# One load of local V, masks first, and rows fetched earlier in a fused sparse-attention and MoE kernel

## The chip, the cores and the metric

The kernel runs on one core of a Trainium2 chip. The metric is device time in microseconds (us) of that core, lower is better. The engines are named as the profile names them: PE (matmul), PEld (its weight load), DVE (VectorE), ACT (ScalarE), POOL (GpSimd) and SP (SyncE, which here only issues transfers). Spans and positions in time come from one profiled execution of each kernel; the time of an execution is 1.7 to 2.0 us longer than its span.

## The reference, cut to what matters

```python
def _attn_ref(q, k, v):                       # each 8 x 8 x 576 x 64, fp32
    scores = scale * q @ k.T
    mask_local   = (rel >= 0) & (rel < 32)    # heads 0 to 3; rel = query - key
    mask_strided = (rel >= 0) & (key % 32 == query % 32)      # heads 4 to 7
    ... softmax over the allowed keys, times v

def _moe_ref(x, w_in, w_out):                 # x: 4608 x 512, d_ff 2048
    r = np.maximum(x @ w_in, 0.0)
    return (r * r) @ w_out
```

Attention of batch b makes 576 rows of x. The 4608 rows of x then go through two matmuls in nine chunks of 512 rows. "MM1 of chunk c" is x @ w_in, "MM2 of chunk c" is the second product. MM1 of chunk c needs the attention of batches up to c, so attention of batch c + 1 is woven between the matmuls of chunk c.

## The kernel before

Heads are handled in pairs, called units: of each batch's four, two are local and two strided. A local unit reads keys in six windows of 128 that overlap by 32. Local V is fetched by POOL's DMAs as those windows, the overlap rows twice:

```python
def load_v_local(u):                          # three DMAs a unit, fp32 to bf16 on the way
    t = vls[v_slot(u)]
    nc.gpsimd.dma_start(out=t[:, :, 0, 0:D], in_=v[b, 2*p:2*p+2, 0:128, :]...)
    for hh in range(2):
        win = bass.AP(src.tensor, src.offset + 64 * D, [[D, 128], [QL * D, NL - 1], [1, D]])
        nc.gpsimd.dma_start(out=t[:, hh, 1:NL, 0:D], in_=win)
```

The rows of q and k of local units come by SP in fp32 and are cast by POOL; those of strided units come by POOL's own DMAs. After the exponential a mask product clears what is not allowed. MM1 ends in a relu on ACT and a square on DVE. These three lines (225, 297 and 188 of the changed kernel) return in the argument:

```python
eng.tensor_tensor(x, x, m..., op=ALU.mult)                 # e <- e, mask: two SBUF inputs
nc.vector.tensor_tensor(g[:, ff, :], r, r, op=ALU.mult)    # square: two SBUF inputs
nc.vector.tensor_copy(o, i)                                # kT <- pt: the transposed k, from PSUM
```

The order of the work is fixed by the program. In the opening:

```python
for n, fn in enumerate(first):          # attention of batch 0
    ...                                 # near its end: rows of batch 1 on ACT's queue
    fn(); tick()
load_v_local(4); cast_qk_local(4, pool2)     # batch 1, on POOL
... load_qk_str(6); load_qk_str(7) ...
for i in range(4): load_w_out(i)
```

and in the stream, a list of groups of four matmuls, into which attention steps and loads are woven:

```python
for c in range(2): all 16 groups of MM1 of chunk c
16 groups of MM2 of chunk 0
for c in range(2, 9): MM1 of chunk c and MM2 of chunk c-1, one group of each in turn
16 groups of MM2 of chunk 8
load_at = {(starts[b - 2] + starts[b - 1]) // 2: b for b in range(2, B)}
```

The softmax here doesn't subtract the row's maximum and nothing guards it: scores larger than these inputs give would overflow.

## Time and profile before

| kernel before | value |
|---|---|
| time, median (lowest to highest of four runs) | 380.87 us (380.09 to 382.98) |
| span of the profiled execution (its time: 381.99 us) | 380.3 us |
| PE busy | 322.9 us, 85% of the span |
| first MM1 of chunk 0 starts at | 33.91 us |
| first MM2 of chunk 1 starts at | 111.55 us |
| from there to the end | 268.8 us |
| mean granted clock | 0.968 |

The two positions are the marks that the rest of this text uses. Up to the second the kernel is opening and start-up; from it on the program repeats one pattern per batch, so the remainder of the span is the steady part plus a tail without attention. The slices, the stretches, the chain and the order of time that carry the reading stand in the prediction. How to read them: a digit of the slices is the busy share of a 40th of the span in tenths, and in the row PEclk the clock granted to PE in tenths of full speed; a row of the stretches gives the stretch, its length, and the busy time of each engine in it; in the order of time a bracket at the end of a row is how long the engine had idled before it, and for what.

One more row of the page, on the transfers:

```profile
DMA packets 50592, 36.10 MB, mean 95 GB/s; under 512 B 28800, under 2 KB 43648, under 8 KB 50560
```

### The profile page before, as it was taken

Reading aid. Unit: us, or ns where it says so; the run is one execution under the profiler, and the core shown is the slowest. Engines: PE = TensorE matmul, PEld = TensorE weight load, DVE = VectorE, ACT = ScalarE, POOL = GpSimd, SP = SyncE. Lnnn points to the kernel's source line nnn. Section 1 sums busy time; section 2 is a strip of 40 time slices with the busy share of each in tenths; the row PEclk is TensorE's granted clock in tenths of the full one; section 3 lists DMA queues with packets and bytes.
Section 4 is the critical chain, followed back from the end, with each engine's and each line's share of the span. In section 5 each row is a group of like instructions: output and inputs, shape, how many; then the busy total and the mean of one; then the engine's idle time right before and its main releaser. Section 6 shows DMA issues by size and latency. Waiting matters only on the chain.

```text
span 380.3 us, 6780 instructions
## 1 busy us (share of the span) xinstructions
PE 322.9 (85%) x2672; PEld 168.3 (44%) x2720; DVE 192.3 (51%) x448; ACT 169.3 (45%) x343; POOL 111.7 (29%) x143
## 2 busy tenths in 40 slices
PE   2277577789999689996999699959999999999995
PEld 1164244345555345543555345534545544444442
DVE  3375458897455447553854386536644632222200
ACT  4231446566335335551555355534555434444421
POOL 8545953991000093007600490019000000000000
PEclk9999779999999989998999899998999999999999
DMA  9999999983110395109800792059100001001012
GB/s 187 122 190 242 197 220 181 184 87 22 57 57 28 98 176 75 47 36 227 94 29 29 204 132 40 29 139 163 55 28 29 29 28 52 33 28 55 29 55 83
DMA packets 50592, 36.10 MB, mean 95 GB/s; under 512 B 28800, under 2 KB 43648, under 8 KB 50560
## 3 DMA queue, kind: packets, MB, share of 16 engines
q0 software_dynamic: 36224, 12.07, 29.0%
q1 hardware_dynamic: 13192, 21.83, 19.5%
q10 hardware_dynamic: 1144, 1.77, 1.9%
q8 instruction: 21, 0.34, 0.4%
q14 instruction: 11, 0.09, 0.1%
HBM read 38.27 MB, written 9.44 MB: 125 GB/s over the span
## 4 chain that ended last, share of the span: by engine, by line
PE 67%; DVE 12%; DMA 11%; ACT 3%; issue 3%; POOL 3%; SPq 0%; POOLq 0%; ACTq 0%
PE ph L284 26%; PE py L299 23%; PE ph L299 7%; DVE g_sb L288 4%; DMA q_st<-in_q_dram 3%; PE pt L167 3%; DMA vl<-in_v_dram 3%; DMA q_s<-in_q_dram 3%; PE pt L202 3%; PE pt L242 3%; ACT r L287 2%; PE pt L265 2%; DMA k_st<-in_k_dram 2%; DVE kT L178 2%; DVE xt L272 2%
## 5 line engine op out<-in xcount | busy, mean ns | idle before, releaser
L284 PE MATMUL ph<-xt,w_in_b 128*128 128x512 bf16 x553 | 150.4, 390 | 3.3 <-DVE xt L272 1.5
L287 ACT ACTIVATE r<-ph 128x512 bf16<-128x512 f32 x144 | 86.1, 598 | 125.5 <-PE ph L284 117.7
L288 DVE TENSOR_TENSOR g_sb<-r 128x512 bf16<-128x512 bf16 x144 | 71.8, 499 | 131.7 <-ACT r L287 131.5
L299 PE MATMUL py<-w_out_b,g_sb 128*128 128x512 bf16 x427 | 114.7, 388 | 1.6 <-issue 0.6
L299 PEld LDWEIGHTS <-g_sb 128*128 128x128 bf16 x576 | 52.2, 99 | 56.2 <-issue 5.0
L284 PEld LDWEIGHTS <-w_in_b 128*128 128x128 bf16 x576 | 51.1, 100 | 48.7 <-issue 4.7
L208 ACT ACTIVATE e<-pt 72x288 bf16<-72x288 f32 (+1 forms) x128 | 48.9, 406 | 29.4 <-PE pt L202 26.4
L91 POOL CAST q_l<-q_st 96x768 bf16<-96x768 f32 x14 | 11.8, 842 | 135.0 <-DMA q_st<-in_q_dram 135.0
L242 PEld LDWEIGHTS <-e 72*128 72x128 bf16 (+1 forms) x448 | 25.8, 104 | 23.5 <-issue 3.3
L176 ACT COPY qT<-pt 128x576 bf16<-128x576 bf16 x32 | 20.4, 637 | 24.5 <-PE pt L167 23.6
L202 PE MATMUL pt<-qT,kT 64*72 64x72 bf16 (+1 forms) x448 | 15.7, 212 | 17.5 <-DVE kT L178 17.0
L118 POOL DMA_DIRECT2D vl<-in_v_dram x32 | 28.4, 897 | 4.4 <-DMA w_out_b<-in_moe_w_out_dram 4.1
L299 PE MATMUL ph<-w_out_b,g_sb 128*128 128x512 bf16 x124 | 29.3, 379 | 0.3
L254 DVE TENSOR_TENSOR x_s<-pt,rinv 72x384 bf16<-72x384 f32 (+1 forms) x48 | 24.5, 509 | 1.7
L167 PE MATMUL pt<-ident,q_l 96*128 96x96 bf16 x96 | 7.8, 225 | 19.8 <-POOL q_l L91 13.6
L202 PEld LDWEIGHTS <-kT 64*72 64x72 bf16 (+1 forms) x448 | 11.1, 111 | 30.1 <-DVE kT L178 24.6
L214 DVE TENSOR_TENSOR e<-e,mask_loc 128x576 bf16<-128x576 bf16 x32 | 19.4, 605 | 7.3 <-POOL mask_loc L392 6.8
L178 DVE COPY kT<-pt 128x576 bf16<-128x576 bf16 x32 | 19.2, 600 | 3.6 <-PE pt L167 3.6
L303 ACT COPY y<-py 128x512 f32<-128x512 f32 x28 | 16.4, 585 | 10.3 <-PE py L299 9.5
L242 PE MATMUL pt<-vs,e 72*128 72x65 bf16 x256 | 16.9, 204 | 2.7 <-DVE e L217 2.7
L131 POOL CAST vs<-v_st 72x1024 bf16<-72x1024 f32 x16 | 18.4, 1174 | 0.0
L254 DVE TENSOR_TENSOR x_l<-pt,rinv 96x384 bf16<-96x384 f32 x32 | 17.7, 553 | 1.1
(43 smaller groups left out, 207.3 us busy)
## 6 DMA issues: line engine op xcount, KB each, us to landing
out_dram<-y SPq DMA_DIRECT2D x36, 256.0 KB
q_st<-in_q_dram SPq DMA_DIRECT2D x14, 288.0 KB
k_st<-in_k_dram SPq DMA_DIRECT2D x14, 288.0 KB
v_st<-in_v_dram SPq DMA_DIRECT2D x14, 288.0 KB
vl<-in_v_dram POOLq DMA_DIRECT2D x32, 80.0 KB, 4.9
q_s<-in_q_dram POOLq DMA_DIRECT2D x16, 144.0 KB, 5.5
k_s<-in_k_dram POOLq DMA_DIRECT2D x16, 144.0 KB, 5.1
w_in_b<-in_moe_w_in_dram POOLq DMA_DIRECT2D x4, 512.0 KB, 7.2
```

The source lines that it names most:

```text
L118: nc.gpsimd.dma_start(out=t[:, hh, 1:NL, 0:D], in_=win)
L176: nc.scalar.copy(o, i)
L178: nc.vector.tensor_copy(o, i)
L202: nc.tensor.matmul(banks[row][half][0:kn, w * i:w * (i + 1)], kT[rows, klo:klo + kn], qT[rows, w * t:w * (t + 1)], start=True, stop=True)
L208: nc.scalar.activation(e[0:kn, lo:lo + S // 2], banks[row][half][0:kn, 0:S // 2], AF.Exp, scale=scale)
L214: nc.vector.tensor_tensor(x, x, mask_loc.rearrange("p t c -> p (t c)"), op=ALU.mult)
L242: nc.tensor.matmul(po[:, n - n0, :], e[0:kn, pos(n):pos(n) + 128], rhs[0:kn, src(n), 0:D + 1], start=True, stop=True)
L254: nc.vector.tensor_tensor(x, po[0:w, 0:m, 0:D], rinv[0:w, 0:m].to_broadcast([w, m, D]), op=ALU.mult)
L284: nc.tensor.matmul(ph, w_in_b[:, kk, 128 * ff:128 * (ff + 1)], xt[kk][:, 512 * c:512 * (c + 1)], start=(kk == 0), stop=(kk == 3))
L287: nc.scalar.activation(r, ph, AF.Relu)
L288: later(1, lambda: nc.vector.tensor_tensor(g[:, ff, :], r, r, op=ALU.mult))
L299: nc.tensor.matmul(py, g[:, ff, 128 * j:128 * (j + 1)], w_out_b[:, ff, :], start=(ff == 0), stop=(ff == 15))
```

## The change: its intent and the diff

Four things are done at once. Local V is loaded once, by SP, in fp32; POOL casts it and copies the 32 overlap rows on chip, so windows become uniform, masks shrink to one narrow tile, and POOL issues fewer DMAs. Masks are built before the casts and weights, and row-0 masks of batch 0 go to POOL, copies and casts of batch 0 to ACT. The rows of a batch are fetched half a chunk pair earlier. And MM2 of chunk 0 goes ahead of MM1 of chunk 1, so that batch 1 has 32 groups of matmuls to hide behind and not 16.

```diff
-    def load_v_local(u):                       # three POOL DMAs
+    def load_v_local(u, eng):
+        t = vl_sts[p]
+        for hh in range(2):
+            eng.dma_start(out=t[32:128, NL * hh:NL * (hh + 1), :],
+                          in_=v[b, 2 * p + hh].rearrange("(t p) d -> p t d", p=QL))
+    def cast_v_local(u):
+        nc.gpsimd.tensor_copy(t[:, :, :, 0:D]..., s["vf"])
+        nc.gpsimd.tensor_copy(t[0:32, :, 1:NL, 0:D], s["vf"][96:128]...[:, :, 0:NL - 1, :])
 ... (keys get 32 zero columns in front: klo = w * t)
         def masks(row):
-            if local: nc.vector.tensor_tensor(x, x, mask_loc...)
-            else:     nc.vector.tensor_tensor(x, x, mask_str.to_broadcast(...))
+            eng = nc.gpsimd if u < 4 and row == 0 else nc.vector
+            eng.tensor_tensor(x, x, m.to_broadcast([kn, n, w]), op=ALU.mult)
 ... (step_E: the xt copies of units 0 to 3 on ACT; casts of units 0 and 1 on ACT)
     def loads(b):
-        load_qk_local, load_v_str; load_v_local(u); cast; load_qk_str(u + 2); load_v_local(u + 1); ...
+        load_qk_local, load_v_local, load_v_str        # all on SP
+        load_qk_str(u + 2); load_qk_str(u + 3)         # POOL issues
+        casts of q, k, local V, strided V              # POOL
 ... (preamble: selects first, then cast_v_local(0), (1), then w_in with strided casts)
-        if n == len(first) - 8: (rows of batch 1 on ACT's queue)
-    load_v_local(4) ... cast_v_str(7)
     for i in range(4):
         load_w_out(i)
+    loads(1)
 ...
-    for i in range(16):
-        add(0, 2, i, ps_h)
+        if c == 0:
+            for i in range(16):
+                add(0, 2, i, ps_h)
-    load_at = {(starts[b - 2] + starts[b - 1]) // 2: b for b in range(2, B)}
+    load_at = {starts[b - 2]: b for b in range(2, B)}
```

More of the change, by code (lines that the diff above doesn't have):

```diff
@@ L59 @@
     ident = singles.tile([128, 128], BF16)
-    mask_loc = singles.tile([128, NL, QL], BF16)
+    mask_loc = singles.tile([128, 1, QL], BF16)
     mask_str = singles.tile([SP_, 1, SP_], BF16)
@@ L63 @@
     vss = [singles.tile([SP_, NBS, VP], BF16, name=f"vs{i}") for i in range(NV)]
+    vl_sts = [singles.tile([128, 2 * NL, D], FP32, name=f"vl_st{i}") for i in range(2)]
+    kTl = [singles.tile([128, 32 + S], BF16, name=f"kTl{i}") for i in range(3)]
     es = [singles.tile([128, 1280], BF16, name=f"e{i}") for i in range(3)]
@@ L106, in v_slot @@
         return (b * 2 + p % 2) % NV
-    def load_v_local(u):
+    def load_v_local(u, eng):
         b, p = units[u]
-        t = vls[v_slot(u)]
-        nc.gpsimd.dma_start(
-            out=t[:, :, 0, 0:D],
-            in_=v[b, 2 * p:2 * p + 2, 0:128, :].rearrange("h p d -> p h d"))
-        for hh in range(2):
-            src = v[b, 2 * p + hh]
-            win = bass.AP(src.tensor, src.offset + 64 * D,
-                          [[D, 128], [QL * D, NL - 1], [1, D]])
-            nc.gpsimd.dma_start(out=t[:, hh, 1:NL, 0:D], in_=win)
-        st.setdefault(u, {})["v"] = t
+        t = vl_sts[p]
+        for hh in range(2):
+            eng.dma_start(out=t[32:128, NL * hh:NL * (hh + 1), :],
+                          in_=v[b, 2 * p + hh].rearrange("(t p) d -> p t d", p=QL))
+        st.setdefault(u, {})["vf"] = t
+    def cast_v_local(u):
+        s = st[u]
+        t = vls[v_slot(u)]
+        nc.gpsimd.tensor_copy(t[:, :, :, 0:D].rearrange("p h t d -> p (h t) d"), s["vf"])
+        nc.gpsimd.tensor_copy(
+            t[0:32, :, 1:NL, 0:D],
+            s["vf"][96:128].rearrange("p (h t) d -> p h t d", h=2)[:, :, 0:NL - 1, :])
+        s["v"] = t
     def load_v_str(u, eng):
@@ L168, in step_T @@
                                 ident[0:w, 0:w])
-        dst = qkT.tile([128, S], BF16, name=f"{name}T")
+        if local and name == "k":
+            full = kTl[u % 3]
+            dst = full[:, 32:32 + S]
+        else:
+            full = dst = qkT.tile([128, S], BF16, name=f"{name}T")
         if local:
@@ L178, in step_T @@
             nc.vector.tensor_copy(o, i)
-        s[name + "T"] = dst
+        s[name + "T"] = full
     def blk_pos(h, j):
@@ L198, in step_S @@
                 t = half * hn + i
-                klo = w * t if not local else max(0, w * t - 32)
+                klo = w * t
                 for row in range(2):
@@ L211, in masks @@
         def masks(row):
-            if local:
-                x = e[:, S * row:S * (row + 1)]
-                nc.vector.tensor_tensor(x, x, mask_loc.rearrange("p t c -> p (t c)"), op=ALU.mult)
-            else:
-                x = e[0:kn, S * row:S * (row + 1)].rearrange("p (t c) -> p t c", c=w)
-                nc.vector.tensor_tensor(x, x, mask_str.to_broadcast([w, n, w]), op=ALU.mult)
+            x = e[0:kn, S * row:S * (row + 1)].rearrange("p (t c) -> p t c", c=w)
+            m = mask_loc if local else mask_str
+            eng = nc.gpsimd if u < 4 and row == 0 else nc.vector
+            eng.tensor_tensor(x, x, m.to_broadcast([kn, n, w]), op=ALU.mult)
         expo(0, 0)
@@ L268, in step_E @@
         dst = xt[p][:, b * S:(b + 1) * S]
+        copy = nc.scalar.copy if u < 4 else nc.vector.tensor_copy
         if local:
-            nc.vector.tensor_copy(dst, px)
+            copy(dst, px)
         else:
-            nc.vector.tensor_copy(dst.rearrange("c (p j) -> c p j", j=NJ),
+            copy(dst.rearrange("c (p j) -> c p j", j=NJ),
                                   px.rearrange("c (j p) -> c p j", j=NJ))
@@ L352, in loads @@
         u = 4 * b
-        load_qk_local(u, nc.sync)
-        load_qk_local(u + 1, nc.sync)
+        for i in range(2):
+            load_qk_local(u + i, nc.sync)
+            load_v_local(u + i, nc.sync)
         load_v_str(u + 2, nc.sync)
         load_v_str(u + 3, nc.sync)
-        load_v_local(u)
-        cast_qk_local(u, pool2)
         load_qk_str(u + 2)
-        load_v_local(u + 1)
-        cast_qk_local(u + 1, pool2)
         load_qk_str(u + 3)
+        for i in range(2):
+            cast_qk_local(u + i, pool2)
+            cast_v_local(u + i)
         cast_v_str(u + 2)
         cast_v_str(u + 3)
-    load_qk_local(0, nc.sync)
-    load_v_local(0)
+    for i in range(2):
+        load_qk_local(i, nc.sync)
+        load_v_local(i, nc.sync)
+    load_qk_str(2)
     make_identity(nc, ident)
-    load_qk_local(1, nc.sync)
-    load_qk_str(2)
     load_v_str(2, nc.sync)
-    load_v_local(1)
     load_v_str(3, nc.sync)
@@ L375 @@
     nc.vector.memset(mask_loc, 1.0)
+    for t in vl_sts:
+        nc.vector.memset(t[0:32], 0.0)
+    for t in kTl:
+        nc.vector.memset(t[:, 0:32], 0.0)
     for t in vls:
         nc.vector.memset(t[:, :, :, D:D + 1], 1.0)
+        nc.vector.memset(t[0:32, :, 0, D:D + 1], 0.0)
     for t in vss:
@@ L381 @@
         nc.vector.memset(e[:, 2 * S:1280], 1.0)
-    tail = mask_loc[:, 1:NL, :]
-    nc.gpsimd.affine_select(out=tail, in_=tail, compare_op=ALU.is_ge, fill=0.0,
-                            base=-1, channel_multiplier=1,
-                            pattern=[[0, NL - 1], [-1, QL]])
-    nc.gpsimd.affine_select(out=tail, in_=tail, compare_op=ALU.is_ge, fill=0.0,
-                            base=32, channel_multiplier=-1,
-                            pattern=[[0, NL - 1], [1, QL]])
-    head = mask_loc[:, 0, :]
-    nc.gpsimd.affine_select(out=head, in_=head, compare_op=ALU.is_ge, fill=0.0,
-                            base=0, channel_multiplier=-1, pattern=[[1, QL]])
-    nc.gpsimd.affine_select(out=head, in_=head, compare_op=ALU.is_ge, fill=0.0,
-                            base=31, channel_multiplier=1, pattern=[[-1, QL]])
+    ml = mask_loc[:, 0, :]
+    nc.gpsimd.affine_select(out=ml, in_=ml, compare_op=ALU.is_ge, fill=0.0,
+                            base=-1, channel_multiplier=1, pattern=[[-1, QL]])
+    nc.gpsimd.affine_select(out=ml, in_=ml, compare_op=ALU.is_ge, fill=0.0,
+                            base=32, channel_multiplier=-1, pattern=[[1, QL]])
     res = singles.tile([SP_, 1, RH], FP32)
@@ L398 @@
                           res.to_broadcast([SP_, NA, RH]))
-    load_w_in(0)
-    cast_v_str(2)
     ms = mask_str[:, 0, :]
@@ L403 @@
                             base=0, channel_multiplier=-1, pattern=[[1, SP_]])
+    cast_v_local(0)
+    cast_v_local(1)
+    load_w_in(0)
+    cast_v_str(2)
     load_w_in(1)
@@ L409 @@
     first = first_steps()
-    cast_qk_local(0, (nc.scalar.copy, nc.vector.tensor_copy))
+    sc2 = (nc.scalar.copy, nc.scalar.copy)
+    cast_qk_local(0, sc2)
     for n, fn in enumerate(first):
         if n == 3:
-            cast_qk_local(1, (nc.scalar.copy, nc.vector.tensor_copy))
-        if n == len(first) - 8:
-            load_qk_local(4, nc.scalar)
-            load_qk_local(5, nc.scalar)
-            load_v_str(6, nc.scalar)
-            load_v_str(7, nc.scalar)
+            cast_qk_local(1, sc2)
         fn()
         tick()
-    load_v_local(4)
-    cast_qk_local(4, pool2)
-    load_v_local(5)
-    cast_qk_local(5, pool2)
-    load_qk_str(6)
-    load_qk_str(7)
-    cast_v_str(6)
-    cast_v_str(7)
     for i in range(4):
         load_w_out(i)
+    loads(1)
     NCH = T // 512
```

## The prediction

> **What bounds the kernel now.** I read the page's slices first, then a table of five stretches, then the chain of waits, then the instructions in order of time around the places where the chain leaves the matmuls. The slices:
>
> ```profile
> PE   2277577789999689996999699959999999999995
> DVE  3375458897455447553854386536644632222200
> PEclk9999779999999989998999899998999999999999
> DMA  9999999983110395109800792059100001001012
> ```
>
> A slice is 9.5 us. The first nine show PE at two to eight tenths with the DMA engines nearly full; after that PE is full but for four slices of 5 or 6 at an even distance, each with a burst of DMA and a clock slice of 8 in it or just behind it. So there are two losses: the opening, and a stall that comes once per batch. The stretches (0 to the first MM1; chunks 0 and 1 of MM1; MM2 of chunk 0; the stream that still carries attention; the stream without it):
>
> ```profile
> core 0: us, PE busy (x) PEld busy (x) DVE busy (x) ACT busy (x) POOL busy (x), PEclk, DMA share, GB/s
> 0.00:33.90 33.90, 14.26 (x196) 10.98 (x198) 18.06 (x52) 10.75 (x23) 19.16 (x32) 1.00 1.12 179
> 33.90:93.20 59.30, 45.57 (x469) 25.35 (x477) 40.81 (x88) 32.30 (x69) 42.30 (x51) 0.91 1.06 159
> 93.20:111.00 17.80, 17.63 (x160) 9.29 (x160) 8.94 (x22) 6.65 (x15) 0.00 (x0) 1.00 0.12 45
> 111.00:307.00 196.00, 176.62 (x1542) 91.52 (x1570) 110.06 (x256) 93.47 (x193) 50.20 (x61) 0.97 0.42 83
> 307.00:380.30 73.30, 68.83 (x313) 31.11 (x318) 14.38 (x33) 26.13 (x44) 0.00 (x0) 1.00 0.12 47
> ```
>
> The last stretch has PE full and no attention in it: a floor that the change doesn't touch. The fourth loses 19.4 us of PE time. The chain names what for:
>
> ```profile
> 129.50 3.29 DMA q_st<-in_q_dram
> 170.04 3.05 DMA q_st<-in_q_dram
> 210.56 3.36 DMA q_st<-in_q_dram
> 251.29 3.25 DMA q_st<-in_q_dram
> ```
>
> Four waits for the first rows of a batch, about 40.5 us apart. The order of time shows how one arises:
>
> ```profile
> 97.92 31.49 SPq L305 DMA_DIRECT2D out_dram<-y  x6
> 129.50 0.38 SPq L83 DMA_DIRECT2D q_st<-in_q_dram  x1
> 132.93 0.81 POOL L91 CAST q_l<-q_st 96x768 bf16<-96x768 f32 x1 [45.65 <-DMA q_st<-in_q_dram]
> 133.80 0.45 PE L167 MATMUL pt<-ident,q_l 96*128 96x96 bf16 x6 [3.45 <-POOL q_l L91]
> ```
>
> The load stands on SP behind stores of y, in program order in the middle of the chunk; the reader should see that POOL had waited 45.65 us, so the cast was ready and the issue was late. In the opening the lines that matter are:
>
> ```profile
> 13.33 0.70 POOL L100 DMA_DIRECT2D k_s<-in_k_dram  x1 [4.09 <-DMA vl<-in_v_dram]
> 15.95 0.46 DVE L214 TENSOR_TENSOR e<-e,mask_loc 128x576 bf16<-128x576 bf16 x1 [6.85 <-POOL mask_loc L392]
> 49.02 0.66 PE L167 MATMUL pt<-ident,q_s 72*128 72x72 bf16 x8 [1.56 <-DMA q_s<-in_q_dram]
> ```
>
> POOL's tenth DMA waits for the second, eight back (local V, in flight from 2.18 to 13.04 us); the masks stand behind it on POOL, and DVE idles 6.85 us for them.
>
> **What the Trainium skill says.** (1) "SBUF — State Buffer", section "Who interferes with whom": a DVE instruction with two SBUF inputs contends with a GpSimd instruction that reads SBUF. The trace agrees: the mask product takes 0.46 us as a rule but 1.89 us at 16.99 and 2.49 us at 65.86 us, both beside POOL casts. (2) "GPSIMD Engine Reference", section 3.1: a two-input elementwise costs about 2.6 cycles per element; at that page's 1.2 GHz, 576 elements make 1.25 us (estimate; before has no such instruction on POOL). (3) "TensorE: Matmul & The Clock Gate", Part 1: after an idle window of about 3.4 us the array runs at half rate. The trace agrees: after the 3.45 us stall the granted clock of 130 to 140 us is 0.83, and matmuls of 512 columns step by about 0.42 instead of 0.216 us. (4) "DMA: Bandwidth & Descriptors", section on queues: each engine consumes a ring in order and takes turns between rings. Before doesn't contradict it; no run isolates it.
>
> **The change, part by part.**
>
> *Rows a chunk ahead.* Loads of batch b move from the middle of the chunk pair to its start, 16 of its 32 matmul groups earlier, so about 17 us earlier. Data, casts and the first transpose take 4.3 us now (129.50 to 133.80). With local V also on SP (two DMAs per unit), the SP burst grows from 6 to 10 issues at about 0.45 us, and POOL first waits a few steps for a free row buffer; call it 10 us together. 17 hides it. One stall costs 3.45 us idle plus the half clock that follows until about 137.6: 3.6 us at half rate, 1.7 us lost, so 5.2 us. Four make 20.8 us. Check: a period is 32 groups x 4 x 0.2155 = 27.6 us, plus a batch's attention on PE. From the chain that is per local unit 0.52 transposes + 0.47 scores + 0.36 + 0.26 = 1.6 us, per strided unit 1.73, so 6.7 us a batch; sum 34.3. Measured: (196.0 - 20.8) / 5 = 35.0. It closes. New stretch: 5 x 35.1 = 175.5 us.
>
> *Opening up to the first MM1 (33.9 now).* Removed from POOL's queue ahead of the masks: the three local-V issues of each of two units (0.87 + 1.77 = 2.6 us a unit) and the 4.09 us wait; the wide selects (0.63 + 0.61) go too. The masks are then ready near 6 instead of 15.9 us. But this is not 10 us won: row-0 masks of units 0 to 3 move to POOL, and there they stand behind all of POOL's preamble: four row issues at 0.73 (2.9), two local-V casts of 0.83 + 0.7 each (3.1, estimated by the q cast of 768 elements), two strided-V casts (2.2), four weight issues (3.1), selects (1.1), so about 12.4 us of work from 1.3 us on, and the casts wait for V: 2.95 MB of batch 0 at about 190 GB/s land by 13 to 15 us. So POOL reaches the first mask at about 20 us and finishes it at 21; now MM of unit 0 starts at 17.72. From there units are faster: DVE loses four masks (1.8 us), four xt copies (2.4) and two casts (1.1) of its roughly 15 us; ACT takes the copies and casts and has about 15 us of work from 2 us on. 21 + 12 = 33 us. I expect 33, a gain of one.
>
> *Stream start.* POOL goes on with four w_out issues, then strided rows of batch 1 (each must wait for the DMA eight back, the w_in loads), then the casts of unit 4. w_in and SP's early loads of batch 1 sum with batch 0 to 7.4 MB, at 205 GB/s 36 us. So the cast comes at about 36 and PE waits some 4 us; strided rows lie in the ring behind 2.1 MB of w_out and cost perhaps 4 more. Then MM1 and MM2 of chunk 0 with batch 1: 34.3 + 2 of small gaps. 33 + 4 + 4 + 36.3 = 77.3 us.
>
> *MM2 first.* Batch 1 gets 32 groups as cover instead of 16, batch 2 gets 16 instead of 32. In MM1 of chunk 1, DVE has 15.1 us for a batch (kT, masks, rinv, x, xt by their rows) + 16 x 0.42 = 21.8, with stretching by POOL 24.5; PE only 20.5. So DVE bounds it: 24.5 us, ending at 101.8. Before, the same work ended at 111.0: 9 us won.
>
> *Copies on chip.* Per batch POOL trades 5.1 us of V issues for 3.1 us of casts; off the path either way.
>
> Sum: 101.8 + 175.5 + 73.3 = 350.6 us of span, and about 1 us from span to time: 352 us.
>
> **Rivals.** (A) POOL becomes the opening's bound: masks at 1.25 us or more, each held by DVE, w_out and casts behind them. For it: POOL's program order and 42.3 of 59.3 us busy already. Against: its work per batch falls. It would make 358 to 366 us. (B) The stalls stay since SP still issues in order, y stores come behind a longer burst, or POOL's row issue waits for a buffer freed late. For: the four stalls are exactly an order problem. Against: 17 us of lead, buffers freed in the first steps of the period. All four kept: 371 us; half of that, 361. (C) w_out is late for MM2 of chunk 0, needed near 57 instead of 93 us (it landed near 65 before, behind small V packets). Up to 8 us more, 360. (D) The opening goes well, batch 1 having arrived long before: no wait at the stream start and the first MM1 near 30: 342.
>
> **Range and chances.** The 20.8 us rest on a wait measured four times; the opening's 9 are a chain of guesses, plus or minus 9. Predicted 352 us, range 344 to 364. Within 2% means above 373.3 us, which needs B in full and nothing won in the opening: faster 0.93, same 0.05, slower 0.02.
>
> **What would show it.** Right: no chain lines of about 3 us for q rows after 100 us; PE slices of 9 there; clock 1.00; first MM1 near 33; MM1 of chunk 2 near 102 with DVE over 85% busy in the stretch before. DVE's 6.85 us for the local mask should be gone, but a wait of PE or DVE for POOL's row-0 mask near 20 us in its place. Wrong: period longer than 36.5 us; PE waiting for w_out; POOL masks far from 1.25 us; first MM1 above 37 or below 29.

## The result, and the profile after

The changed kernel took 365.07 us (median of four runs, 363.83 to 369.91; the last of these counts as slow), the kernel before 380.87. The ratio is 0.957 (95% interval 0.951 to 0.962). Ratios here are the mean time of one kernel's fast runs over that of the other's in the same rounds, so they are not quite the ratio of the medians. Executions over 1.5% slower than the fastest of the same kernel are left out of the means. The kernel is faster, but by 15.8 us where 29 were predicted, and 365.07 lies 1.07 above the upper end of the range.

| | before | predicted | after |
|---|---|---|---|
| first MM1 of chunk 0 | 33.9 | 33 | 36.0 |
| MM1 and MM2 of chunk 0 | | 44.3 | 51.9 |
| MM1 of chunk 1 | | 24.5 | 27.3 |
| start of the steady part | 111.0 | 101.8 | 115.2 |
| five batches of the stream | 196.0 | 175.5 | 175.3 |
| tail without attention | 73.3 | 73.3 | 73.3 |
| span | 380.3 | 350.6 | 363.8 |

The slices of the kernel after:

```profile
PE   2247776999778999999999999899999999999995
DVE  4126166555887656665666666656545622222200
PEclk9999988899999999999999999999999999999999
DMA  8999999212995330494059306900000010010012
```

From slice 14 on PE reads 9 but for one 8 and the last slice, and the granted clock 9 throughout: the four dips of before are gone. But the first twelve slices are no fuller: their PE digits add up to 76, before's to 79. The stretches (to the first MM1; MM1 of chunk 0; its MM2; MM1 of chunk 1; the stream with attention; the tail):

```profile
core 0: us, PE busy (x) PEld busy (x) DVE busy (x) ACT busy (x) POOL busy (x), PEclk, DMA share, GB/s
0.00:36.00 36.00, 14.30 (x197) 10.95 (x199) 13.63 (x51) 14.22 (x29) 21.36 (x33) 1.00 1.08 209
36.00:69.20 33.20, 25.09 (x185) 12.40 (x188) 16.35 (x31) 15.40 (x33) 22.28 (x28) 0.90 0.95 169
69.20:87.90 18.70, 17.99 (x186) 9.71 (x186) 9.84 (x25) 6.44 (x15) 0.67 (x1) 1.00 0.23 58
87.90:115.20 27.30, 21.95 (x264) 12.63 (x266) 22.78 (x53) 17.19 (x37) 12.15 (x14) 1.00 0.99 206
115.20:290.50 175.30, 168.85 (x1541) 89.55 (x1570) 106.03 (x255) 93.65 (x193) 44.72 (x54) 1.00 0.37 82
290.50:363.80 73.30, 68.86 (x313) 31.11 (x318) 14.36 (x33) 26.14 (x44) 0.00 (x0) 1.00 0.13 47
```

The fifth row is the success: 175.30 us, with PE busy for 168.85 of them. In the second row PE is busy for 25.09 of 33.20 us, though the matmuls of MM1 in it amount to 16 groups x 4 x 0.2155 = 13.8 us. Attention comes on top: 185 - 64 = 121 of its matmuls, where a batch has 196 (all of batch 0's stand in the first row), so 4.2 us at the prediction's 6.7 a batch. That makes 18.0 us, which is also what the third row's like work keeps PE busy (17.99). So 8.1 us are idle in the second row and some 7 are lost while busy. In the fourth row DVE has the least slack, 22.78 of 27.30 us. The chain of waits has only two transfers in it, both in the opening and none after 100 us:

```profile
4.44 10.24 DMA vl_st<-in_v_dram
...
20.69 17.34 DMA w_in_b<-in_moe_w_in_dram
```

The order of time, cut to the rows that matter in the opening:

```profile
21.44 2.52 POOL L225 TENSOR_TENSOR e<-e,mask_loc 128x576 bf16<-128x576 bf16 x2
22.79 0.51 PE L250 MATMUL pt<-vl,e 128*128 128x65 bf16 x6 [7.44 <-POOL e L225]
...
38.61 0.68 POOL L102 DMA_DIRECT2D k_s<-in_k_dram  x1 [1.55 <-DMA w_in_b<-in_moe_w_in_dram]
39.29 0.84 POOL L93 CAST q_l<-q_st 96x768 bf16<-96x768 f32 x1
40.19 0.66 PE L173 MATMUL pt<-ident,q_l 96*128 96x96 bf16 x6 [2.71 <-POOL q_l L93]
40.65 1.91 PE L293 MATMUL ph<-xt,w_in_b 128*128 128x512 bf16 x4
...
46.65 1.04 PE L293 MATMUL ph<-xt,w_in_b 128*128 128x512 bf16 x4
...
58.43 2.86 DVE L297 TENSOR_TENSOR g_sb<-r 128x512 bf16<-128x512 bf16 x1
58.64 0.84 POOL L93 CAST q_l<-q_st 96x768 bf16<-96x768 f32 x1
...
61.71 0.47 PE L212 MATMUL pt<-qT,kT 64*72 64x72 bf16 x16 [3.18 <-DVE kT L188]
```

Here are the three kinds of loss. First, POOL reaches the first mask at 21.44 us, and PE idles 7.44 us before it can use it. It is late through POOL's fixed order: the cast of the second unit's V waited 3.97 us for data until 14.82, and then three more casts and four weight issues stood ahead of the mask. Second, the cast for unit 4, which PE awaits until 40.19, stands behind the strided k issue, which itself had waited 1.55 us for a w_in transfer. Third, the square of 58.43 us lasts 2.86 us instead of 0.42, while POOL casts one piece after another at 58.64, 59.41, 60.18 and 61.07; the copy of kT behind it in DVE's order is late, and PE idles 3.18 us. The two rows of groups of four matmuls show the rest: 1.91 us at 40.65 and 1.04 at 46.65 for the same work, so half rate at the first. It holds from the first matmul of MM1 at 35.99 to about 45.7 us, so it began before the wait of 2.71 us, and it comes back behind idle times of 1.36 us (at 52.57) and 3.18 us (at 61.71). A row that doesn't help is the clock's: it reads 9 in the first five slices, to 45 us, while the group at 40.65 ran at half rate.

### The profile page after: what moved, and what is told of

It is laid out like the page before. It is cut to its first block, busy times and chain, and to the rows that moved or that the text cites. A ratio compares the mean times of both kernels' runs of the same rounds, so it can differ in the third digit from the quotient of the medians.

```text
span 363.8 us, 6813 instructions
## 1 busy us (share of the span) xinstructions
PE 317.0 (87%) x2672; PEld 166.4 (46%) x2720; DVE 183.0 (50%) x447; ACT 173.0 (48%) x349; POOL 101.2 (28%) x129
## 3 DMA queue, kind: packets, MB, share of 16 engines
q0 software_dynamic: 10880, 8.92, 16.2%
## 4 chain that ended last, share of the span: by engine, by line
PE 74%; DVE 10%; DMA 8%; ACT 3%; issue 2%; POOL 2%; SPq 1%; POOLq 0%; ACTq 0%
PE ph L293 31%; PE py L308 25%; PE ph L308 7%; DMA w_in_b<-in_moe_w_in_dram 5%; DVE g_sb L297 4%; PE pt L173 3%; PE pt L250 3%; PE pt L212 3%; DMA vl_st<-in_v_dram 3%; ACT r L296 3%; PE pt L273 2%; DVE xt L281 1%; DVE x_l L262 1%; DVE kT L188 1%; DVE x_s L262 1%
## 5 line engine op out<-in xcount | busy, mean ns | idle before, releaser
L308 PE MATMUL py<-w_out_b,g_sb 128*128 128x512 bf16 x427 | 111.5, 379 | 1.6 <-issue 0.6
L102 POOL DMA_DIRECT2D q_s<-in_q_dram x16 | 11.2, 698 | 99.0 <-PE pt L173 77.6
L250 PEld LDWEIGHTS <-e 72*128 72x128 bf16 (+1 forms) x448 | 24.9, 102 | 26.0 <-POOL e L225 7.6
L261 DVE RECIPROCAL rinv<-pt 96x6 f32<-96x6 f32 (+2 forms) x80 | 14.7, 183 | 14.2 <-PE pt L250 14.1
L250 PE MATMUL pt<-vl,e 128*128 128x65 bf16 x192 | 12.1, 201 | 8.8 <-POOL e L225 7.4
L121 POOL CAST vl<-vl_st 128x768 bf16<-128x768 f32 x16 | 13.9, 869 | 14.9 <-DMA vl_st<-in_v_dram 14.8
L137 POOL CAST vs<-v_st 72x1024 bf16<-72x1024 f32 x16 | 17.2, 1093 | 2.9 <-DMA v_st<-in_v_dram 2.5
L188 DVE COPY kTl<-pt 128x576 bf16<-128x576 bf16 x16 | 12.0, 750 | 9.4 <-PE pt L173 9.4
L250 PE MATMUL pt<-vs,e 72*128 72x65 bf16 x256 | 16.0, 200 | 0.0
L225 DVE TENSOR_TENSOR e<-e,mask_str 72x576 bf16<-72x576 bf16 x30 | 15.1, 503 | 1.4 <-ACT e L218 1.2
```

Of the source, the lines that this page charges most:

```text
L137: nc.gpsimd.tensor_copy(t[:, :, 0:D], s["vf"].rearrange("p h (j d) -> p (h j) d", d=D))
L250: nc.tensor.matmul(po[:, n - n0, :], e[0:kn, pos(n):pos(n) + 128], rhs[0:kn, src(n), 0:D + 1], start=True, stop=True)
L308: nc.tensor.matmul(py, g[:, ff, 128 * j:128 * (j + 1)], w_out_b[:, ff, :], start=(ff == 0), stop=(ff == 15))
```

## The experiments

Twelve kernels were run, each on one chip with its own runs of the kernel before (medians of 379.7 to 381.2 us), and each for 3 rounds. All gave correct results. One table first, as it separates the two parts of the change by itself. The last two columns cut each span at the start of the first MM2 of chunk 1, which can be found in every trace and lies 0.2 to 0.6 us behind the start of the steady part in the table above.

| kernel | time, us | ratio to before (95%) | opening | from there on |
|---|---|---|---|---|
| before | 380.87 | 1 | 111.6 | 268.8 |
| after | 365.07 | 0.957 (0.951 to 0.962) | 115.4 | 248.4 |
| prefetch_only | 362.05 | 0.951 (0.945 to 0.956) | 110.2 | 250.9 |
| loads_mid | 385.05 | 1.014 (1.007 to 1.020) | 114.3 | 269.0 |
| masks_dve | 364.43 | 0.956 (0.949 to 0.963) | 117.4 | 247.5 |
| mm1_first | 367.97 | 0.968 (0.962 to 0.973) | 117.6 | 248.0 |
| rows_first | 360.50 | 0.949 (0.944 to 0.955) | 109.7 | 248.6 |
| rows_first_masks_dve | 354.48 | 0.935 (0.927 to 0.942) | 103.8 | 247.9 |
| prefetch_mm2 | 357.92 | 0.942 (0.935 to 0.949) | 108.1 | 249.1 |
| square_psum | 370.09 | 0.972 (0.961 to 0.983) | 118.2 | 248.9 |
| interleave | 357.19 | 0.942 (0.936 to 0.948) | 105.5 | 249.2 |
| act_casts | 355.29 | 0.934 (0.928 to 0.940) | 105.8 | 247.9 |
| v_windows | 358.77 | 0.942 (0.933 to 0.952) | 105.6 | 248.9 |
| w_in_early | 357.78 | 0.941 (0.937 to 0.944) | 106.9 | 248.0 |

The last column falls into two groups: 269 where rows are fetched late, 247 to 251 where they are fetched early. All else the experiments move is in the opening.

### prefetch_only: the early rows alone

The theory to be tested: the early rows are the whole gain, and the rest of the change costs time in the opening. Its rival: the parts each bring some of it. The kernel before gets one line of the change:

```diff
-    load_at = {(starts[b - 2] + starts[b - 1]) // 2: b for b in range(2, B)}
+    load_at = {starts[b - 2]: b for b in range(2, B)}
```

> The kernel before with one part of the change alone: the loads of a batch moved from the middle of a chunk pair to its start. Theory 1 (the four stalls of 5.2 us come from the late issue alone): about 361 us, no stall of 3 us after 100 us, and so as fast as the whole change or faster, since the opening is then left as it was. Theory 2 (the early load only helps together with V on the SP queue, because three V issues per unit on POOL hold the casts back): at most half of the stalls go, 370 us or more.

Measured: 362.05 us. The stream with attention (columns as in the stretches above):

```profile
108.90:288.00 179.10, 169.92 (x1551) 89.97 (x1578) 112.17 (x257) 94.17 (x194) 51.62 (x61) 1.00 0.47 91
```

179.1 us against 196.7 in the kernel before, cut at the same matmul, and no wait for q rows in the chain after 100 us. So one line brings as much as the whole change: the ratio is 0.951 where the full change has 0.957, with intervals that overlap. The other parts bring 2.5 us behind the mark (250.9 to 248.4) and lose 5.2 ahead of it (110.2 to 115.4). In the stream of prefetch_only four squares last 1.71 to 2.47 us beside POOL's casts, in that of the changed kernel none over 1.31; that fits the 2.5 us, but no run isolates it.

### loads_mid: all of the change but the early rows

```diff
-    load_at = {starts[b - 2]: b for b in range(2, B)}
+    load_at = {(starts[b - 2] + starts[b - 1]) // 2: b for b in range(2, B)}
```

> The changed kernel with the loads put back to the middle of the chunk pair. Theory 1: the four stalls come back, 365 + 20 = 385 us, slower than before by what the opening lost. Theory 2 (the rest of the change carries a good part of the gain): 372 us or less.

Measured: 385.05 us, slower than before by 1.4% (interval 0.7 to 2.0%). The chain of waits has its four lines back, a batch apart as ever:

```profile
132.67 3.46 DMA q_st<-in_q_dram
...
173.31 3.32 DMA q_st<-in_q_dram
...
213.79 3.35 DMA q_st<-in_q_dram
...
254.31 3.57 DMA q_st<-in_q_dram
```

Take the early rows from the changed kernel, and it is worse than the one it came from. The theory stands from both sides.

### masks_dve: row-0 masks of batch 0 back on DVE

Rival A of the prediction names POOL's order as the opening's bound. If its mask products are the cause, DVE should do better.

```diff
-            eng = nc.gpsimd if u < 4 and row == 0 else nc.vector
+            eng = nc.vector
```

> The changed kernel with the row-0 masks of units 0 to 3 back on DVE. Theory A (POOL's serial preamble holds unit 0): the first use of e moves from 22.8 to about 16 us, the first MM1 from 36 to about 31 us. If nothing else stands behind it, the total falls by 4 to 5 us to 360; if the casts of batch 1, which wait on POOL for the w_in loads until 38 us, are the next bound, at most 2 us are gained. Theory B (DMA volume bounds the opening): first MM1 stays within 1 us and the total at 365.

Measured: 364.43 us, no gain, although the first MM1 starts 5.4 us sooner, at 30.63. Two rows of the order of time say where it went:

```profile
36.19 0.68 POOL L102 DMA_DIRECT2D q_s<-in_q_dram  x1 [4.00 <-DMA w_in_b<-in_moe_w_in_dram]
...
40.81 0.66 PE L173 MATMUL pt<-ident,q_l 96*128 96x96 bf16 x6 [8.70 <-POOL q_l L93]
```

POOL, rid of its masks, reaches the strided row issues earlier and waits there for w_in, 2.33, 3.28, 4.00 and 2.37 us one after the other. The local casts stand behind all four, and PE waits 8.70 us for the first at 40.81, where it had waited 2.71 at 40.19 before. So the masks had hidden a second bound that ends at the same time. The wait was moved, not removed.

### rows_first: the rows of batch 1 ahead of w_out

POOL's waits for w_in show a rule of this program, read off from which transfer ended which wait: each POOL DMA was held until the POOL DMA eight places before it had landed. In masks_dve the four parts of w_in land at 27.23, 31.21, 35.60 and 38.66 us, and the four row issues start at 27.51, 31.50, 36.19 and 39.24. The trace's semaphores show where the rule comes from: the program signals the landing of POOL's DMAs on eight semaphores in turn, and each held DMA waits for the one that it is to use again. With four w_out issues ahead, the strided rows come eight behind w_in. Put the rows first, and they come eight behind small transfers that landed long ago.

```diff
+    loads(1)
     for i in range(4):
         load_w_out(i)
-    loads(1)
```

> The changed kernel with the loads and casts of batch 1 ahead of the w_out issues in POOL's order. The strided row issues then have fewer than eight POOL DMAs since w_in began to wait for, and the cast of unit 4 no longer stands behind the landing of w_in (38.05 us). Theory 1 (program order on POOL holds batch 1): cast of unit 4 near 35 us, the 2.7 us wait of PE gone, about 362 us. Rival (data volume: the rows or w_in are late anyway, or w_out now is): 365 us or more, with a new wait of PE for w_out near 69 us.

Measured: 360.50 us. The four strided issues now run from 32.02 to 34.79 without a wait, and the cast follows them:

```profile
34.79 0.84 POOL L93 CAST q_l<-q_st 96x768 bf16<-96x768 f32 x1
```

That is 4.5 us sooner than in the changed kernel (39.29). The 2.71 us wait of PE is gone, and the opening ends 5.7 us sooner (115.4 to 109.7), more than the wait alone: MM1 of chunk 0 takes 27.95 us instead of 33.20, although a stretched product still costs PE 4.08 us in it, at 56.56. It confirms that w_out stood in the way by its places in POOL's order: the last part of w_in lands at the same time as before (38.16 and 38.03 us), but the cast no longer stands behind it. As the bytes of w_out move back too, the run doesn't tell what they cost the rest of the opening.

### rows_first_masks_dve: both

With the second bound gone, the masks on DVE should pay.

```diff
-            eng = nc.gpsimd if u < 4 and row == 0 else nc.vector
+            eng = nc.vector
+    loads(1)
     for i in range(4):
         load_w_out(i)
-    loads(1)
```

> Both undone at once: masks of units 0 to 3 on DVE and batch 1 ahead of w_out on POOL. Theory 1: the first MM1 at about 31 us as with the masks alone, but without the 8.7 us wait that swallowed it there; 5 to 9 us below the changed kernel, 356 to 360 us. Rival (DMA volume bounds the opening): PE now waits for w_in, w_out or batch 2's rows instead, 363 us or more.

Measured: 354.48 us, ratio 0.935: with act_casts below (355.29 us, 0.934) the best of the kernels here, 10.6 us below the changed kernel by the medians of two chips. The first three stretches, cut as for the kernel after:

```profile
0.00:30.20 30.20, 14.28 (x197) 10.96 (x199) 16.44 (x55) 14.34 (x29) 20.19 (x33) 1.00 1.09 211
30.20:58.20 28.00, 21.69 (x187) 11.29 (x190) 16.41 (x31) 15.12 (x33) 14.73 (x19) 0.94 1.17 216
58.20:76.90 18.70, 17.99 (x185) 9.71 (x185) 9.80 (x25) 6.43 (x16) 5.08 (x6) 1.00 0.47 96
```

30.2, 28.0 and 18.7 us stand against 36.0, 33.2 and 18.7. Alone, the mask's edit gave nothing; on top of the other it gives 6.0 us. One large wait is left:

```profile
46.39 3.08 DVE L225 TENSOR_TENSOR e<-e,mask_loc 128x576 bf16<-128x576 bf16 x1
...
50.75 0.70 PE L212 MATMUL pt<-qT,kT 64*72 64x72 bf16 x16 [4.09 <-DVE kT L188]
```

DVE's mask product of 0.45 us lasts 3.08, beside POOL casts from 46.78 to 51.97 us.

### square_psum: a square with one input from PSUM

This tests the third kind of loss. The rival explanation is that the square waits for ACT or for its buffer and that POOL's casts lie beside it by chance. If two SBUF inputs are the cause, a form with one of them in PSUM keeps its length beside the same casts.

```diff
-        later(1, lambda: nc.vector.tensor_tensor(g[:, ff, :], r, r, op=ALU.mult))
+        later(1, lambda: nc.vector.scalar_tensor_tensor(g[:, ff, :], ph, 0.0, r,
+                                                        op0=ALU.max, op1=ALU.mult))
```

> The changed kernel with the square taken as max(ph, 0) * r, one input from PSUM and one from SBUF, in place of r * r with two inputs from SBUF. If the 2.8 us square at 58.4 us is held by POOL's casts because both engines read SBUF through one shared interface, no square is longer than about 1 us beside POOL casts and the 3.2 us wait of PE at 61.7 us is gone: 2 to 4 us faster, unless the slower form (estimate 0.6 to 0.7 in place of 0.42 us) makes DVE the bound of MM1 of chunk 1. If something else held it, the long ones stay.

Measured: 370.09 us, ratio 0.972, unclear by the 2% line. Its fast runs, 366.98 to 371.16 us, all lie above those of the changed kernel, 363.83 to 365.74, on another chip. A square, a cast and a mask product:

```profile
60.62 0.69 DVE L297 SCALAR_TENSOR_TENSOR g_sb<-ph,r 128x512 bf16<-128x512 f32 x1
60.84 0.83 POOL L93 CAST k_l<-k_st 96x768 bf16<-96x768 f32 x1
...
63.62 0.86 DVE L225 TENSOR_TENSOR e<-e,mask_str 72x576 bf16<-72x576 bf16 x1
```

All 144 squares take 0.67 to 0.69 us, beside casts or not, while a mask product among the same casts, with both inputs in SBUF, still stretches to 0.86, and another, at 91.08, to 2.34. The changed kernel agrees without any edit: its products with one input from PSUM (line 262) keep their 0.55 us in all 16 cases beside POOL's casts and masks. PE's wait at that place fell from 3.18 us to 0.59, and MM1 of chunk 0 ends at 67.67 instead of 69.24. But each square is 0.27 us longer than an undisturbed one, and the stretch of MM1 of chunk 1 up to the mark, where DVE already has the least slack, grows from 27.5 to 31.7 us. Not all of that is the square's: behind the mask product of 2.34 us PE waits 2.89 us at 94.44, where it waited 0.47 in the changed kernel. So two SBUF inputs are the cause of the stretching; the cure as a whole doesn't pay, and how much of its price the slower square bears isn't isolated.

### mm1_first and prefetch_mm2: what MM2 of chunk 0 first is worth

One kernel takes the order back in the changed kernel, the other adds it to the early rows alone:

```diff
 mm1_first (from the changed kernel)
-        if c == 0:
-            for i in range(16):
-                add(0, 2, i, ps_h)
+    for i in range(16):
+        add(0, 2, i, ps_h)
 prefetch_mm2 (from the kernel before): the early load_at, and
-    for i in range(16):
-        add(0, 2, i, ps_h)
+        if c == 0:
+            for i in range(16):
+                add(0, 2, i, ps_h)
```

> The changed kernel with MM2 of chunk 0 behind MM1 of chunk 1 again. If squeezing batch 2 into 16 groups costs the 3 us that the chunk took over its estimate (27.5 against 24.5), about 362 us. If the cover that batch 1 gains from 32 groups is worth more, 367 to 370 us, with batch 1's stretch DVE-bound instead.

> The kernel before with two parts: the early loads and MM2 of chunk 0 ahead of MM1 of chunk 1; V windows, masks and the opening's order as before. If the parts add up (MM2 first was worth some 3 us in the changed kernel), 359 us. If MM2 first only helps where batch 1's rows are late, 362 us or more. If w_out, which landed near 65 us there, is late for it: 365 us.

Measured: 367.97 and 357.92 us. Taken back, the opening grows from 115.4 to 117.6; added, it shrinks from 110.2 to 108.1. By the spans, the order is worth 2 us ahead of the mark in either surrounding; by the times of different chips it is 2.9 and 4.1, with intervals that touch or overlap. So it seems to pay, but not the 9 us that the prediction drew from it. prefetch_mm2 also answers rival C: it needs w_out at 59.04 us for MM2 of chunk 0, with the four w_out issues starting at 43.88, and PE doesn't wait for it. And it is 7 us faster than the full change, with none of its V, mask and copy parts.

### interleave and act_casts: against the stretched product

Both start from rows_first_masks_dve and try to break up POOL's burst of casts, which stretches DVE's product to 3.08 us.

```diff
 interleave: for i in 0, 1 (in loads)
-    load_qk_str(u + 2); load_qk_str(u + 3); then all casts
+    cast q; issue strided q; cast k; issue strided k; cast local V
 act_casts: from batch 2 on
-    cast_qk_local(u + i, pool2)
+    later(n + ..., lambda i=i: cast_qk_local(u + i, sc2))      # on ACT, n groups later
```

> The version with both undone (rows_first_masks_dve), and POOL's casts of local q and k alternate with the issues of the strided rows. There PE lost 4.1 us at 50.75 us to a mask product of 3.0 us on DVE beside six POOL casts back to back. If DVE can take the shared interface whenever POOL is in an instruction that reads no SBUF operand, no DVE product beside POOL exceeds about 1.3 us, and the total falls by 2 to 5 us to 350 to 353 us. If POOL's DMA issues hold the interface as the casts do, or the q rows now come late, no change (354 to 356 us).

> The same version with the local q and k casts of batches 2 to 7 on ACT, a fixed number of groups after the loads. If POOL's casts holding DVE's two-input products is what the opening still loses, the 4 us wait goes and the total is 350 to 353 us; ACT pays 3.3 us per batch where it is half idle. If ACT is held by rows that have not landed, its exponentials come late and the total is 356 us or more.

Measured: 357.19 and 355.29 us; neither beats rows_first_masks_dve (ratios 0.942 and 0.934 against 0.935). In both the product got shorter, as aimed at: the longest is 1.69 us with interleave and 1.18 with act_casts. With interleave PE then waits 2.75 us at 45.37 and 1.98 at 103.17 in other places, and POOL's issue of strided q waits 7.16 us for PE to free a buffer: a miss. With act_casts PE's wait of 4.09 us falls to 1.67, and two new ones come: 1.03 us for ACT's relu at 56.19, and w_out is late after all:

```profile
61.95 0.38 PE L308 MATMUL ph<-w_out_b,g_sb 128*128 128x512 bf16 x1 [1.16 <-DMA w_out_b<-in_moe_w_out_dram]
```

So 2.4 us won and 2.2 lost, and the opening by the mark is no shorter (105.8 against 103.8, on another chip).

### v_windows and w_in_early: the V part, and the weights

v_windows is rows_first_masks_dve with local V as before, in windows by POOL's DMAs; w_in_early issues all of w_in ahead of the V casts, so that nothing on POOL waits for it later.

```diff
 v_windows
-            load_v_local(u + i, nc.sync)  ... cast_v_local(u + i)
+            load_v_local(u + i)                     # three POOL DMAs
 w_in_early
+    for i in range(4):
+        load_w_in(i)
     cast_v_local(0)
     cast_v_local(1)
-    load_w_in(0) ... load_w_in(3)
```

> The version with both undone, and the V part undone as well: overlapping V windows by POOL's DMAs, the wide mask, no zero columns. If loading V once is worth what its fewer packets and issues suggest, this is slower: six V issues stand ahead of the masks in POOL's queue and later ones wait for the DMA eight back, 359 to 364 us. If the V part only moves work from DMA to POOL and the SP burst, 353 to 356 us.

> The version with both undone, and the four w_in issues ahead of the first local V cast, where POOL idles 3 us. It asks whether POOL's order still costs something in the opening or whether the bytes now do. Order: w_in lands earlier, w_out is issued without its 1.2 us wait, and the total is 350 to 353 us. Bytes: w_in takes its share from the rows of units 0 and 1, the first MM1 moves from 30.2 to 33 us or later, and the total is 355 us or more.

Measured: v_windows 358.77 us (356.06 to 366.52, the last of these slow), ratio 0.942 with an interval from 0.933 to 0.952 that overlaps with that of rows_first_masks_dve. POOL issues V's windows behind w_in:

```profile
29.11 0.86 POOL L118 DMA_DIRECT2D vl<-in_v_dram  x1 [2.68 <-DMA w_in_b<-in_moe_w_in_dram]
```

By the spans the V part is worth 2.8 us (354.5 against 351.7), by the times it isn't separated from nothing; that stays open. w_in_early gave 357.78 us, no gain over rows_first_masks_dve: the intervals overlap (0.937 to 0.944 against 0.927 to 0.942), and its span is 3.2 us longer (354.9 against 351.7). Its w_in is in flight together with V:

```profile
19.65 0.83 POOL L121 CAST vl<-vl_st 128x768 bf16<-128x768 f32 x1 [8.51 <-DMA vl_st<-in_v_dram]
```

V of the second unit reaches its cast at 19.65 us instead of 14.8, and the first MM1 starts at 32.11 instead of 30.17. So the bytes on their way hold the opening too, not only POOL's order; in the changed kernel that shows as the 3.97 us that POOL waits for the same V.

## Why the prediction was right or wrong, point by point

**The stalls (right; the exact figure in part by luck).** 175.5 us were predicted for the stream and 175.3 measured. loads_mid shows that nothing is won there without the early rows, and the clock behaved as argued: 0.97 in that stretch before, 1.00 after. But prefetch_only has the early rows alone, and behind the mark they take off 17.9 us (268.8 to 250.9), so 4.5 a stall and not 5.2. The last 2.5 us came with the other parts, for which the prediction reckoned nothing in the stream. Rival B, that stalls stay, fell in all kernels with early rows.

**Up to the first MM1 (short by 3.0).** The row "21 + 12 = 33" came out as 22.79 + 13.2 = 36.0. POOL's mask cost what was estimated from "GPSIMD Engine Reference", section 3.1 (about 2.6 cycles per element of a two-input operation): 2.52 us for two, against 1.25 each. The place of it in POOL's order was 1.4 us late (21.44, "about 20"). The units behind it were faster than before, as argued, 13.2 us against 16.2 from the first use of e (33.91 less 17.72), but not 12. That masks on POOL bound this part, as rival A had it, is shown by masks_dve, which took 5.4 us off it.

**Stream start (short by 7.6): the step that failed.** The prediction had 34.3 us of work, 4 for the cast, 4 for strided rows behind w_out, and 2 of small gaps: 44.3. Measured were 35.9 of work, 8.1 idle in MM1, some 7 in slow matmuls and 0.8 over in MM2, together 51.9 (rounding 0.1). The work is 1.6 more than predicted, as the two rows hold 185 + 186 - 128 = 243 attention matmuls, 1.24 batches and not one: batch 2 had begun. Of the idle part, the cast's wait was 2.71 us, so right in kind; the strided rows' 4 us did not come at all; in their place came 3.18 us from a stretched square and 1.36 and 0.69 from other DVE work. So the waits came to less than predicted, and the 7 us of slow matmuls are the term that was missing. The prediction had priced a stall in the stream with its slow clock, 3.45 idle and 1.7 lost, and left that second part out in the opening, where there are more idle times. The table of stretches shown in it had the figure: in chunks 0 and 1 before, PE is busy for 45.57 us with 2 x 13.8 us of MM1 and 469 - 128 = 341 attention matmuls, 1.74 batches or 11.7 us, so 39.3 of work.

**MM2 first (short by 2.8 in MM1 of chunk 1, and wrong as a gain).** DVE does bound that stretch: it is busy for 22.78 of 27.30 us, which is 83% and just under the 85% given as a sign, and over half of the stretch's chain of waits (some 58%) is DVE's work. It was mis-sized: 24.5 was to hold the stretching by POOL, but squares of 1.33 and mask products of 1.17 us came with it. The order itself is worth about 2 us by mm1_first and prefetch_mm2. The "9 us won" that the prediction writes down here is no price of the order: it compares an opening with underestimated losses with a real one.

**The rivals.** Rival A, POOL as the opening's bound, was given 358 to 366 us; the kernel took 365.07. The experiments bear it out, with two corrections: not only masks but the order of issues counts, and part of it acts through DVE, whose products POOL's casts stretch. Rival C didn't come about in the changed kernel (w_out was there in time); it appeared only once the opening was shorter, as the 1.16 us of act_casts. Rival D, 342 us, was not reached by any kernel. Two small slips: the totals of rival B, 371 and 361, are spans and not times, and from span to time it is 1.7 to 2.0 us, not 1.

**The range** had 344 to 364 around 352. The opening's error of plus or minus 9 was the right kind of doubt and too small: 13.4 us came (115.2 against 101.8), all on one side: 3.0, 7.6 and 2.8.

## What to carry to other kernels

A one-line change of when a load is issued gave as much as all four parts here, since the other three, taken together, cost in the opening more than they brought; so try each part alone before they are merged. When moving work to an engine that is idle on average, write down what stands ahead of it in that engine's program order, transfers it waits for included, and what its memory reads do to its neighbour. And take a price for matmuls from a stretch with the same idle times, for here 8.1 us of idle time in the start-up came with some 7 more of slow matmuls.

## What the Trainium skill lacked or had wrong

- "SBUF — State Buffer", sections "SBUF: two separate sides" and "Who interferes with whom": that a DVE instruction with two SBUF inputs contends with GpSimd reads is borne out (square_psum: 0.67 to 0.69 us with one input in PSUM, against up to 2.86 with both in SBUF). But the page has the lock held for the whole of one instruction, by whichever starts first, and doesn't say what happens between POOL instructions that follow one another. Here the square started at 58.43 us and ended at 61.29, behind three casts of 0.83 us without a gap, from 58.64 to 61.01; in v_windows one started at 112.53 and ended at 116.51, behind five, to 116.24 (the first had begun before it). So the wait was for the whole row of casts. (The square started first by the record in the first case, but POOL's spans are rough, so that this contradicts the page isn't shown.)
- "TensorE: Matmul & The Clock Gate", Part 1: half rate after idle time agrees (1.91 against 1.04 us for four matmuls). The page warns that a trace's clock events are unreliable; a case of it here is that the profile's clock row read 9 up to 45 us, with matmuls at half rate from 35.99 to 45.7, so before that the duration of matmuls has to be read and not the clock. What the page lacks is how busy a window of about 3.4 us must be to count as busy: at 52.61 half rate set in behind an idle time of only 1.36 us, with PE busy for 1.73 of the 3.60 us before.
- No page that was read tells that a POOL DMA in such a program is held until the POOL DMA eight places before it has landed. It cost 4.09 us in the kernel before, and 2.33, 3.28, 4.00 and 2.37 us in masks_dve. By the trace's semaphores the program makes that rule and not the chip: POOL's DMAs signal on eight semaphores in turn.
